# Transfers of q, k and V moved to GpSimd's queue, low parts one step later, and work respread in an attention and expert kernel

## The chip, the cores and the metric

One core of a Trainium2 chip runs the whole program. The core has five engines that run side by side and wait for one another by semaphores: TensorE (PE in the profile; its weight loads are listed as PEld), VectorE (DVE), ScalarE (ACT), GpSimd (POOL) and SyncE (SP), which here only issues transfers between device memory and the core's SBUF. The metric is device time in microseconds from start to end of the program; smaller is better. TensorE's results land in PSUM, which has eight banks per partition; VectorE and ScalarE read them there, GpSimd does not.

## What is computed

Attention for 2 batches, 8 heads, 576 positions and 64 columns per head, with a position bias from a small network; then two mixtures of experts over the 1152 rows of the result, the second with its own gate.

```python
scores = scale * np.matmul(q, k.transpose(0, 1, 3, 2))
h = np.maximum(x @ w1 + b1, 0.0)          # x: log distances over log positions
scores = scores + (h @ w2).transpose(2, 0, 1)[None]
attn = softmax(scores); out = attn @ v
# experts, layer 1 (4) and layer 2 (8); D = 512, F = 1024
for e in range(E):
    h = np.maximum(x @ w1[e], 0.0)
    out += p[:, e:e + 1] * (h @ w2[e])
# layer 2: p from logits x @ w_gate: exp(logits - max), then 8 rounds that
# divide by row sums and by column sums
```

All of it is float32. The expert products are made from split operands: a high part (the value rounded to the form that TensorE takes at full rate) and a low part (the value less its high part), three products for each pair.

## The kernel before

**Attention** runs in 36 units. A unit `u` is a block of 128 query rows (`t`, 0 to 4; block 4 holds the last 64 rows of both batches), a pair of heads (`p`) and, for blocks 0 to 3, a batch (`b`). The order is block 0 (units 0 to 7), block 4 (8 to 11), then 1, 2, 3. The loop over `k` is a software pipeline written out by hand: iteration `k` issues for unit `k` the scores (`emit_S`, line 346), their maximum with the bias added (`emit_max`, line 364 on VectorE) and the exponentials (`emit_exp`, ScalarE); for unit `k-1` the reciprocal of the row sums (`emit_recip2`, line 387, whose input `emit_recip` has GpSimd add, line 383) and its copy `spread` on GpSimd; for `k-2` the transposes (`emit_T`, and `emit_tail` for the last 64 columns and `spread`) and their evacuations (`emit_evac`, lines 416 and 418); for `k-3` the product with V (`emit_P`, line 435) into `po`; for `k-4` the scaled result (`emit_x`, line 445, VectorE). Each engine executes what is issued for it in that order.

**Bias.** 36 groups of 16 rows are made beside the units: hidden values `hids` (mostly VectorE, line 283), a product (line 297), a scaled evacuation to one of three places of `bsts` (ScalarE, line 326), a store to device memory `bd` (SP, line 329); `load_bias` (lines 255 and 256) reads it back shifted as `bt`, in two transfers, four for block 4. Eight groups come before everything else, three more before the first unit, then one per unit up to unit 24.

**Loads.** SP issues all transfers in program order: `load_q` (two per head pair and block, 20 calls), `load_k` (two, 8 calls), `load_v` (three, 4 calls, with a memset on GpSimd), bias stores and loads, and from unit 24 the expert weights (`load_raw`). A transfer whose buffer isn't free, or whose source isn't written, holds up those behind it.

**Experts.** A step `n` is a layer, an expert, a chunk of rows (five row tiles, or four) and a quarter of F. `L1` makes the first product of step `n+1` by Strassen's scheme in seven products and a closing part (`m1`, `m6`, `m2`, `m7`, `m5`, `m4`, `m3`, `last`) over three PSUM banks A, B, C, with VectorE's sums (`u2`, `u3`, line 655) between; a bank is taken again only when it has been read. `L2` makes the second product of step `n` into `y` (line 726). `step` interleaves them in slots, and `at(n, slot, ...)` hangs other work into a slot. `split_raw` splits weights (line 162 on GpSimd, sums on VectorE).

**Operands.** `pieces` makes the seven combinations of the rows that the scheme needs (`X`). Each piece is three parts; a part makes sums on VectorE and calls `split`, which copies the high part on ScalarE (line 99) and at once has another engine subtract for the low part (line 100). Layer 1's first chunk is made in iterations 16 to 34 of attention, its second chunk in steps 0 and 1, layer 2's after layer 1.

**Between the layers** each finished row tile is transposed (`transposed`), gated (`gate`) and split; `sinkhorn` finds the largest logit (`largest`, `turned`, `largest_of_all` at line 831), broadcasts it by a product (`to_all`, line 835), exponentiates, and runs eight rounds.

Of the kernel before, what the change touches and what calls it, by code (L numbers as in the profile page):

```python
# [9 lines left out]
F32 = mybir.dt.float32  # L10
F32R = mybir.dt.float32r
AF = mybir.ActivationFunctionType
ALU = mybir.AluOpType
# [12 lines left out]
WARM = 10  # L26
# [22 lines left out]
def attn_moe_moe(ctx: ExitStack, tc: tile.TileContext, pack, keep, rel, qT, kT, vT, w, out):  # L49
# [40 lines left out]
    def pieces(layer, c):  # L90

        n = CHUNKS[c][1]
        for i in XA:
            X[layer, c, i] = xpools[c].tile([128, 2, 2, n], F32R, tag=f"x{c}{i}", name=f"x{layer}{c}{i}")

        def split(i, src, o, w, lo):
            x = X[layer, c, i]
            hi = x[:, 0, :, o:o + w]
            sc.activation(out=hi, in_=src, func=AF.Copy)
            lo.tensor_tensor(out=x[:, 1, :, o:o + w], in0=src, in1=hi.bitcast(F32), op=ALU.subtract)  # L100

        def piece(k1, c1, k2, c2, w, o):
            h1, h2 = col_tile(k1)[:, :, c1:c1 + w], col_tile(k2)[:, :, c2:c2 + w]
            a11, a12, a21, a22 = h1[:, 0:2], h1[:, 2:4], h2[:, 0:2], h2[:, 2:4]
            t1, t2 = (g1.tile([128, 2, 128], F32, tag=f"t{i}", name=f"t{i}_{layer}{k1}")[:, :, 0:w] for i in range(2))

            def part1(eng, other):
                eng.tensor_tensor(out=t1, in0=a21, in1=a22, op=ALU.add)
                eng.tensor_tensor(out=a21, in0=a11, in1=a21, op=ALU.subtract)
                eng.tensor_tensor(out=t2, in0=t1, in1=a11, op=ALU.subtract)  # L110
                split("A11", a11, o, w, other)

            def part2(eng, other):
                split("A12", a12, o, w, eng)
                eng.tensor_tensor(out=a12, in0=a12, in1=t2, op=ALU.subtract)
                split("A22", a22, o, w, other)
                split("S1", t1, o, w, eng)

            def part3(eng, other):
                split("S2", t2, o, w, eng)  # L120
                split("S3", a21, o, w, eng)
                split("S4", a12, o, w, eng)

            return [part1, part2, part3]

        return [piece(*x) for x in CHUNKS[c][2]]


    NP = F // 256
# [46 lines left out]
    def attention(moe):  # L176
# [17 lines left out]
        V = [atb.tile([128, 5, 2 * B * D], F32, name=f"V{p}") for p in range(4)]  # L194

        def load_v(p):
            sy.dma_start(out=V[p][:, 0:4, :], in_=vT[p, 0:512].rearrange("(j p) x -> p j x", p=128))
            gp.memset(V[p][:, 4, :], 0.0)
            for h in range(2):
                to, of = (x.rearrange("p (b h d) -> p h b d", b=2, h=2)[:, h] for x in (V[p][:, 4, :], vT[p, 512:576]))  # L200
                sy.dma_start(out=to[64 * h:64 * h + 64], in_=of)

        bdram = [dram.tile([H, (128 if t < 4 else 64) + 1, W], F32, name=f"bd{t}") for t in range(5)]

# [7 lines left out]
        def load_k(p, b):  # L212
            i = 2 * p + b
            r = xa.tile([128, 1280], F32, tag=f"x0{XA[i % 4]}", name=f"kr{p}{b}")[:, 0:S]
            for h in range(2):
                sy.dma_start(out=r[64 * h:64 * h + 64], in_=kT[p, b, 0:64, S * h:S * h + S])
            rawk[p, b] = r

        def prep_k(p, b, hi):
# [9 lines left out]
        def load_q(t, p):  # L229
            r = ata.tile([128, 256], F32, tag="qraw", name=f"qr{t}{p}", bufs=3)  # L230
            for h in range(2):
                sy.dma_start(
                    out=r[64 * h:64 * h + 64].rearrange("p (b c) -> p b c", b=2),
                    in_=qT[t, p, 0:64].rearrange("p (b h c) -> p h b c", b=2, h=2)[:, h],
                )
            rawq[t, p] = r
# [214 lines left out]
        kq = [(p, b) for p in range(4) for b in range(2)]  # L451

        gp.memset(ones, 1.0)
        for _ in range(WARM):
            pe.matmul(out=po_all[:, 0, 0:128], lhsT=ones, rhs=ones, start=True, stop=True)
        sy.dma_start(out=cst, in_=pack)
        sy.dma_start(out=T, in_=rel)
        load_q(*tps_[0])
# [43 lines left out]
                load_k(*kq[4])  # L502
                load_q(*tps_[2])

        load_bias(*tps_[0])
        load_bias(*tps_[1])
        load_k(*kq[5])
        load_q(*tps_[3])
        prep_q(*tps_[1])
        prep_k(*kq[2], sc)  # L510
        for _ in range(3):
            groups(1)
            hids(4)
        prep_k(*kq[3], sc)

        ti, work, first_split = 0, [], None
        for k in range(U + 3):
            first = False
            if k < U:
                t, p, b = units[k]  # L520
                first = b == 0
                if first:
                    ti = tps_.index((t, p))
                emit_S(k)
                emit_max(k)
                if k > 0:
                    emit_recip2(k - 1)
                if k >= 4:
                    emit_x(k - 4)
            elif k == U:  # L530
                emit_recip2(k - 1)
                emit_x(k - 4)
                st_sc.close()
                st_a.close()
                moe.open1()
                first_layer = moe.L1(0)
                for fn in first_layer[0:3]:
                    fn()
            if k < U:
                emit_exp(k, 0)  # L540
            if k >= 2 and k - 2 < U:
                emit_T(k - 2)
                emit_evac(k - 2, 0, sc)
            if k < U:
                emit_exp(k, 1)
            if k >= 2 and k - 2 < U:
                emit_evac(k - 2, 2, sc)
            groups(1)
            if k >= 2 and k - 2 < U:
# [27 lines left out]
                ve.reciprocal(psm, psm)  # L577
                ve.tensor_tensor(out=p1, in0=dp, in1=psm.unsqueeze(2).to_broadcast([128, NTT, E1]), op=ALU.mult)
            if k == 15:
                work = [part for p_ in pieces(1, 0) for part in p_]  # L580
            if work and (15 < k < 19 or 22 < k):
                work.pop(0)(ve, gp)
            if k == 24:
# [18 lines left out]
    class Moe:  # L602
# [169 lines left out]
        def turn(self, n, c):  # L772
# [7 lines left out]
            if c == 0:  # L780
                for i, k in enumerate(tiles):
                    self.at(n + 1, 1 + i, lambda k=k: self.transposed(k, "y4"))
                    self.at(n + 1, 2 + i, lambda k=k: self.gate(k, "y4"), False)
                self.at(n + 1, 7, make)
                for i in range(15):
                    self.at(n + 1 + (i + 7) // 8, (i + 7) % 8, lambda i=i: self.parts[i // 3][i % 3](ve, gp))
            else:
                for i, (slot, tag) in enumerate(((6, "A"), (7, "B"), (8, "C"), (8, "A"))):
                    self.at(n + 1, slot, lambda k=tiles[i], tag=tag: self.transposed(k, tag))
                for i, k in enumerate(tiles):  # L790
                    self.at(n + 2, 6 + i, lambda k=k, i=i: self.gate(k, "ABCA"[i]))
                self.at(n + 2, 9, make)
                for i in range(6):
                    self.at(n + 3, i, lambda i=i: self.parts[i // 3][i % 3](ve, gp))
                self.sinkhorn(n + 5)

        def transposed(self, k, tag):
# [17 lines left out]
        def sinkhorn(self, n0):  # L815
# [53 lines left out]
            self.at(n0 - 2, 4, largest)  # L869
            self.at(n0 - 2, 7, turned, False)  # L870
            self.at(n0 - 2, 7, largest_of_all)
            self.at(n0 - 2, 9, to_all, False)
            self.at(n0 - 2, 9, exps)
            for i in range(SINKHORN):
                self.at(n0 + i // 2, 2 + 4 * (i % 2), sums, False)
                self.at(n0 + i // 2, 2 + 4 * (i % 2), lambda i=i: over_cols(i))
# [25 lines left out]
                gran.pop(self.gidx(n))  # L902

        def run(self):
            work = [part for p_ in pieces(1, 1) for part in p_]
            for i, part in enumerate(work):
                self.at(i // 3, 2 + 2 * (i % 3), lambda part=part: part(ve, gp))
            for n in range(self.N):
                self.step(n)

# [73 lines left out]
```

## Time and profile before

| | us |
|---|---|
| median of three runs | 1388.31 (1388.0 to 1389.45) |
| the profiled execution | 1387.5 |
| its span, first to last instruction | 1385.7 |
| TensorE busy in the span | 1339.5 (97%) |
| VectorE, ScalarE, GpSimd busy | 783.9, 517.5, 390.2 |
| mean granted TensorE clock | 0.993 of full speed |

A busy TensorE is not TensorE at its peak: matmuls are pipelined, and their ends are modelled. The granted clock has two levels here, 1.0 (2.4 GHz) and 0.5 (1.2 GHz). Times in a timeline count from the start of the span.

### The profile page before, as it was taken

The page shows a single profiled execution, that of the slowest core. Times are in us where ns is not written, and L with a number is a line of the kernel's source. Part 1 is how long each engine was busy: PE and PEld are TensorE (multiplying, and loading weights), DVE is VectorE, ACT ScalarE, POOL GpSimd, SP SyncE. Part 2 cuts the span into 40 slices and gives each one's busy share as a digit, 9 for nine tenths or more (in the row PEclk, how much of TensorE's full clock was granted, in tenths as well). Part 3 has the DMA queues.
Part 4 walks back from the last instruction along what each step waited for, and adds up shares of the span by engine and source line. Part 5 has one row for each costly group of instructions (what it writes and reads, how often), then busy time and mean ns, then how long its engine had stood idle before and what let it go on. Part 6 is the DMA issues. An engine that isn't in the chain of part 4 may idle for free.

```text
span 1385.7 us, 22442 instructions
## 1 busy us (share of the span) xinstructions
PE 1339.5 (97%) x8763; PEld 1167.2 (84%) x8763; DVE 783.9 (57%) x1775; ACT 517.5 (37%) x1226; POOL 390.2 (28%) x391
## 2 busy tenths in 40 slices
PE   7889888999999999999999999999999999999998
PEld 3576677899899898889888888898988988988987
DVE  7667778454464463585474473664544734635643
ACT  6768774334142241343243241331321422413311
POOL 0111134044062160144062260340530612604400
PEclk9899999999999999999999999999999999999999
DMA  7775521011021020011021030020110210301110
GB/s 208 197 180 143 159 66 61 31 61 62 0 87 37 0 94 29 1 61 62 1 92 31 14 97 12 31 92 0 62 61 1 92 31 26 97 1 35 58 39 31
DMA packets 42170, 84.68 MB, mean 61 GB/s; under 512 B 10320, under 2 KB 17744, under 8 KB 42064
## 3 DMA queue, kind: packets, MB, share of 16 engines
q1 hardware_dynamic: 42064, 83.24, 19.7%
q8 instruction: 69, 1.13, 0.3%
q14 instruction: 37, 0.30, 0.1%
HBM read 69.97 MB, written 13.25 MB: 60 GB/s over the span
## 4 chain that ended last, share of the span: by engine, by line
PE 84%; DVE 7%; ACT 3%; DMA 3%; issue 1%; POOL 1%; SPq 1%; ACTq 0%; DVEq 0%; POOLq 0%
PE y L726 41%; PE B L647 16%; PE A L647 10%; PE C L647 10%; PE po L435 2%; PE sc L346 2%; DVE s L364 2%; ACT s L377 1%; PE bps L297 1%; PE tp L409 1%; DMA bd<-bsts 1%; DMA rawb<-in_w 1%; ACT bsts L326 1%; DMA bt<-bd 1%; ACT at L418 1%
## 5 line engine op out<-in xcount | busy, mean ns | idle before, releaser
L726 PE MATMUL y<-gb,h 128*128 128x512 f32 x2592 | 714.7, 396 | 0.0
L726 PEld LDWEIGHTS y<-gb,h 128*128 128x128 f32 x2592 | 451.5, 188 | 56.0 <-issue 0.2
L162 POOL TENSOR_TENSOR gb<-rawb,gb 128x512 fp32r<-128x512 f32 x94 | 126.7, 1361 | 637.9 <-ACT gb L161 630.8
L655 DVE TENSOR_TENSOR u<-B,s 128x320 f32<-128x320 f32 (+1 forms) x192 | 87.7, 457 | 311.9 <-PE B L647 311.7
L658 ACT ACTIVATE h<-c 128x320 fp32r<-128x320 f32 (+1 forms) x288 | 119.6, 439 | 385.3 <-DVE c L655 383.8
L661 DVE SCALAR_TENSOR_TENSOR h<-c,h 128x320 fp32r<-128x320 f32 (+1 forms) x288 | 170.1, 607 | 53.0 <-ACT h L658 48.1
L162 POOL TENSOR_TENSOR ga<-rawa,ga 128x512 fp32r<-128x512 f32 x94 | 120.5, 1300 | 5.9 <-ACT ga L161 5.8
L655 DVE TENSOR_TENSOR c<-C,u 128x320 f32<-128x320 f32 (+1 forms) x192 | 87.5, 456 | 60.7 <-PE C L647 57.1
L162 POOL TENSOR_TENSOR ga<-wt,ga 128x512 fp32r<-128x512 f32 x94 | 105.4, 1141 | 36.1 <-ACT ga L161 19.2
L669 ACT ACTIVATE s<-A 128x320 f32<-128x320 f32 (+1 forms) x96 | 39.5, 411 | 173.0 <-PE A L647 173.0
L658 ACT ACTIVATE h<-A 128x320 fp32r<-128x320 f32 (+1 forms) x96 | 39.1, 407 | 146.1 <-PE A L647 145.9
L655 DVE TENSOR_TENSOR c<-B,s 128x320 f32<-128x320 f32 (+1 forms) x96 | 43.9, 458 | 82.0 <-PE B L647 80.8
L161 ACT ACTIVATE gb<-rawb 128x512 fp32r<-128x512 f32 x96 | 60.1, 627 | 73.0 <-DMA rawb<-in_w 73.0
L377 ACT ACTIVATE s<-s,stat 128x576 f32<-128x576 f32 x72 | 55.4, 769 | 42.1 <-DVE stat L364 41.2
L435 PEld LDWEIGHTS po<-at,V 128*64 128x64 f32 x800 | 39.3, 137 | 33.7 <-DVE rows L445 32.5
L647 PE MATMUL A<-x20A,ga 128*128 128x320 f32 x384 | 66.9, 309 | 0.0
L647 PE MATMUL B<-x20S,ga 128*128 128x320 f32 x384 | 66.8, 309 | 0.0
L647 PE MATMUL C<-x20S,ga 128*128 128x320 f32 x384 | 66.7, 309 | 0.0
L647 PEld LDWEIGHTS B<-x20S,ga 128*128 128x128 f32 x384 | 61.6, 188 | 5.8
L647 PEld LDWEIGHTS C<-x20S,ga 128*128 128x128 f32 x384 | 61.3, 188 | 5.8
L647 PEld LDWEIGHTS A<-x20A,ga 128*128 128x128 f32 x384 | 61.4, 188 | 5.6
L435 PE MATMUL po<-at,V 128*64 128x128 f32 (+1 forms) x800 | 47.5, 267 | 16.1 <-DVE rows L445 16.1
(173 smaller groups left out, 1904.8 us busy)
## 6 DMA issues: line engine op xcount, KB each, us to landing
rawa<-in_w SPq DMA_DIRECT2D x48, 512.0 KB, 4.0
rawb<-in_w SPq DMA_DIRECT2D x48, 512.0 KB, 4.9
bd<-bsts SPq DMA_DIRECT2D x36, 295.5 KB, 3.4
bt<-bd SPq DMA_DIRECT2D x16, 512.0 KB, 4.3
qr<-in_qT SPq DMA_DIRECT2D x40, 64.0 KB, 3.0
kr<-in_kT SPq DMA_DIRECT2D x16, 144.0 KB, 3.2
V<-in_vT SPq DMA_DIRECT2D x4, 512.0 KB, 4.8
bt<-bd SPq DMA_DIRECT2D x8, 256.0 KB, 4.0
```

The source lines that it names most:

```text
L161: sc.activation(out=z(0), in_=src, func=AF.Copy)
L162: lo.tensor_tensor(out=z(1), in0=src, in1=z(0).bitcast(F32), op=ALU.subtract)
L346: pe.matmul(out=o[h][:, j, 0:288], lhsT=qq[t, p][d, x, 128 * bb:128 * bb + 128], rhs=kk[p, bb][d, y, 288 * j:288 * j + 288], start=i == 0, ...
L364: ve.tensor_tensor_reduce(out=s.rearrange("p (a j) -> p a j", a=2), in0=scps.pop((u, h))[:, :, 0:288], in1=bt[t, p][:, S * h:S * h + S].re ...
L377: sc.activation(out=s, in_=s, func=AF.Exp, scale=-1.0, bias=stat[u][:, h:h + 1], accum_out=stat[u][:, 2 + h:3 + h],)
L435: pe.matmul(out=o[64 * h:64 * h + 64, c0:c0 + n], lhsT=V[p][:, j, col:col + D], rhs=rhs, start=j == 0, stop=j == 4,)
L647: pe.matmul(out=ban[o], lhsT=a, rhs=x[:, z, k, :], start=not more and i == 0, stop=i == 5, skip_group_check=more,)
L655: ve.tensor_tensor(out=t[o], in0=ban[a], in1=t[b], op=ALU.add)
L658: sc.activation(out=h[f][:, 0, half, :], in_=src, func=AF.Relu)
L661: ve.scalar_tensor_tensor(out=h[f][:, 1, half, :], in0=src, scalar=0.0, in1=h[f][:, 0, half, :].bitcast(F32), op0=ALU.max, op1=ALU.subtract,)
L669: sc.activation(out=t["s1"], in_=ban["A"], func=AF.Copy)
L726: pe.matmul(out=self.y[t], lhsT=a, rhs=x, start=g == 0 and f == 0 and i == 0, stop=g == NP - 1 and f == 1 and i == 2,)
```

## The change

Transfers of q, k and V are issued by GpSimd instead of SP. In `pieces` the subtraction for a low part is put aside (`pending`) and issued at the start of the next part (`flush`), so that there is one closing part more; the copies are spread otherwise over the three parts. In the first units TensorE gets products of ones whose result nobody reads (`busy`): eight before unit 0, six after the scores of units 0, 1 and 2. `emit_x` stands ahead of `emit_S`. Once all bias groups are made, one evacuation moves ahead of the second exponential. The first two bias loads come after bias group 8. The parts of layer 1's second chunk go from steps 0 and 1 to steps 1 and 2, with low parts on VectorE alone. The broadcast of the largest logit and the exponentials move from step 34 to step 35, slot 9.

```diff
@@ pieces
+        pending = []
         def split(i, src, o, w, lo):
             sc.activation(out=hi, in_=src, func=AF.Copy)
-            lo.tensor_tensor(out=x[:, 1, :, o:o + w], in0=src, in1=hi.bitcast(F32), op=ALU.subtract)
+            pending.append(lambda: lo.tensor_tensor(out=x[:, 1, :, o:o + w], in0=src, in1=hi.bitcast(F32), op=ALU.subtract))
+        def flush(eng=None, other=None):
+            while pending:
+                pending.pop(0)()
             def part1(eng, other):
+                flush()
                 ...
+                split("A12", a12, o, w, eng)
                 split("A11", a11, o, w, other)
+                split("S1", t1, o, w, eng)
             def part2(eng, other):
-                split("A12", a12, o, w, eng)
+                flush()
                 eng.tensor_tensor(out=a12, in0=a12, in1=t2, op=ALU.subtract)
+                split("S2", t2, o, w, eng)
                 split("A22", a22, o, w, other)
-                split("S1", t1, o, w, eng)
             def part3(eng, other):
-                split("S2", t2, o, w, eng)
+                flush()
                 split("S3", a21, o, w, eng)
                 split("S4", a12, o, w, eng)
-        return [piece(*x) for x in CHUNKS[c][2]]
+        return [part for x in CHUNKS[c][2] for part in piece(*x)] + [flush]
@@ load_v, load_k, load_q (each transfer)
-            sy.dma_start(...)
+            gp.dma_start(...)
@@ before the units
-        load_bias(*tps_[0])
-        load_bias(*tps_[1])
         load_k(*kq[5])
         load_q(*tps_[3])
         prep_q(*tps_[1])
         prep_k(*kq[2], sc)
-        for _ in range(3):
+        for g in range(3):
             groups(1)
             hids(4)
+            if g == 0:
+                load_bias(*tps_[0])
+                load_bias(*tps_[1])
+        busy(8)
         prep_k(*kq[3], sc)
@@ the units
+                if k >= 4:
+                    emit_x(k - 4)
                 emit_S(k)
+                if k < 3:
+                    busy(6)
                 emit_max(k)
                 if k > 0:
                     emit_recip2(k - 1)
-                if k >= 4:
-                    emit_x(k - 4)
             ...
                 emit_evac(k - 2, 0, sc)
+                if made == NGR:
+                    emit_evac(k - 2, 2, sc)
             if k < U:
                 emit_exp(k, 1)
-            if k >= 2 and k - 2 < U:
+            if k >= 2 and k - 2 < U and (k - 2, 2) in tps:
                 emit_evac(k - 2, 2, sc)
@@ Moe.turn: 16 parts instead of 15 for the first chunk, 7 instead of 6 for the second
@@ sinkhorn
-            self.at(n0 - 2, 9, to_all, False)
-            self.at(n0 - 2, 9, exps)
+            self.at(n0 - 1, 9, to_all, False)
+            self.at(n0 - 1, 9, exps)
@@ run
-            for i, part in enumerate(work):
-                self.at(i // 3, 2 + 2 * (i % 3), lambda part=part: part(ve, gp))
+            for i, part in enumerate(pieces(1, 1)):
+                self.at(*((1, 1 + 3 * i) if i < 3 else (2, 2 * i - 5)), lambda part=part: part(ve, ve))
```

## Rows read from the trace of the kernel before

**Rows 1.** Busy time by stretch: stretch, its length, engines (instructions), clock, DMA share, GB/s.
```profile
0.00:58.00 58.00, 42.64 (x353) 23.73 (x354) 41.52 (x108) 37.49 (x77) 4.40 (x17) 0.88 0.71 204
...
156.00:202.00 46.00, 37.26 (x442) 31.31 (x444) 37.17 (x120) 33.32 (x96) 16.07 (x34) 1.00 0.36 111
202.00:250.00 48.00, 41.95 (x280) 36.53 (x277) 38.20 (x69) 22.11 (x54) 19.27 (x18) 0.96 0.21 66
...
575.00:725.00 150.00, 143.89 (x849) 127.17 (x848) 99.97 (x268) 62.43 (x162) 59.23 (x56) 0.99 0.15 47
...
sum 1385.00, PE 1339.53 PEld 1167.19 DVE 783.95 ACT 517.52 POOL 390.19; mean PE 167.44 PEld 145.90 DVE 97.99 ACT 64.69 POOL 48.77
```

**Rows 2.** Who waited for whom: us in total, times, longest us.
```profile
PE po L435 <- DVE rows L445: 16.1, 18, 2.2
...
DVE s L364 <- PE sc L346: 11.5, 15, 1.8
```

**Rows 3.** Timeline 26 to 37 us: start, length, what, idle before and its releaser.
```profile
26.50 1.05 PE L346 MATMUL sc<-kk,qq 64*128 64x288 f32 x11 [0.92 <-ACT bsts L326]
...
28.53 1.24 SPq L232 DMA_DIRECT2D qr<-in_qT  x2
29.34 0.76 DVE L364 CUSTOM_DVE_ANT_0 s<-sc,bt 128x576 f32<-128x576 f32 x1 [1.44 <-DMA bt<-bd]
29.87 6.50 SPq L329 DMA_DIRECT2D bd<-bsts  x4
...
34.78 1.05 ACT L326 ACTIVATE bsts<-bps,cst 128x16 f32<-128x16 f32 x2 [3.01 <-DMA bd<-bsts]
...
35.88 1.81 PE L346 MATMUL sc<-kk,qq 64*128 64x288 f32 x11 [3.03 <-ACT bsts L326]
```

**Rows 4.** Timeline of a later unit: eight transposes, of the fill products' shape.
```profile
62.81 1.04 PE L409 MATMUL tp<-kept,s 128*128 128x128 f32 x8
```

**Rows 5.** Busy time in the stretch of the lower clock, columns as in the first group.
```profile
28.00:41.60 13.60, 8.40 (x51) 4.60 (x52) 7.24 (x21) 6.42 (x14) 1.57 (x4) 0.50 0.70 201
```

**Rows 6.** GpSimd's sums (ns min/median/max), then sums and tails of units 0 and 4.
```profile
L383 POOL TENSOR_SCALAR stat<-stat x36: 213/219/625, 31.9 to 202.7; 128x2 f32<-128x2 f32 x36
...
31.86 0.62 POOL L383 TENSOR_SCALAR stat<-stat 128x2 f32<-128x2 f32 x1 [30.94 <-ACT s L377]
...
41.28 0.42 PE L398 MATMUL sc<-kept,spread 128*128 128x128 f32 x1
...
57.05 0.35 POOL L383 TENSOR_SCALAR stat<-stat 128x2 f32<-128x2 f32 x1 [1.11 <-ACT s L377]
...
62.70 0.27 PE L398 MATMUL sc<-kept,spread 128*128 128x128 f32 x1
```

**Rows 7.** Timeline, VectorE's maxima of units 10 and 12.
```profile
84.20 0.76 DVE L364 CUSTOM_DVE_ANT_0 s<-sc,bt 128x576 f32<-128x576 f32 x1 [2.97 <-DMA bt<-bd]
...
96.11 0.76 DVE L364 CUSTOM_DVE_ANT_0 s<-sc,bt 128x576 f32<-128x576 f32 x1 [2.91 <-DMA bt<-bd]
```

**Rows 8.** Timeline, steps 0 and 1 of the expert layers.
```profile
226.22 1.14 PE L647 MATMUL B<-x10A,ga 128*128 128x320 f32 x6 [1.71 <-DVE u L655]
...
240.04 1.45 POOL L162 TENSOR_TENSOR ga<-rawa,ga 128x512 fp32r<-128x512 f32 x1
240.29 1.48 DVE L108 TENSOR_TENSOR t<-rows 128x256 f32<-128x256 f32 x1
...
243.51 1.94 PE L647 MATMUL B<-x10A,ga 128*128 128x320 f32 x6 [3.31 <-DVE u L655]
...
244.53 0.42 DVE L115 TENSOR_TENSOR rows<-rows,t 128x256 f32<-128x256 f32 x1
```

**Rows 9.** Groups in 157 to 202 us: busy, mean ns, idle before.
```profile
L435 PE MATMUL po<-at,V 128*64 128x128 f32 x212 | 14.0, 278 | 8.7 <-DVE rows L445 8.7
```

**Rows 10.** Timeline of TensorE around the broadcast of the largest logit.
```profile
662.63 0.38 PE L835 MATMUL B<-m,ones 1*128 1x1 f32 x2 [1.84 <-DVE m L831]
662.94 1.65 PE L726 MATMUL y<-gb,h 128*128 128x512 f32 x3
```

## What I predict, before the result is known

> **What bounds the kernel now.** I read the table by stages first: busy time of each engine in stretches of the span [rows 1]. TensorE is busy for 1339.5 of 1385.7 us; of the 46 us that it stands still, 36 lie in four places: 58.0 - 42.6 = 15.4 us in the start of attention, 46.0 - 37.3 = 8.7 us in its last units, 48.0 - 42.0 = 6.0 us at the entry to the first expert layer, 150.0 - 143.9 = 6.1 us in the passage between the layers. The long expert stretches behind them have nothing to give. Next, who ended these waits [rows 2]: the largest single one is the attention product `po` waiting 16.1 us, in 18 pieces, for VectorE's line 445 (`emit_x`). Last the timeline of each place, in the order below. The change touches all four.
>
> **Start, unit 0: SP relieved.** The store of bias group 8 leaves at 29.87 us, because two bias loads, two transfers of k and two of q stand before it in SP's queue; ScalarE then waits 3.01 us for that store's buffer (`bsts` has three places) and S(1) on TensorE 3.03 us for ScalarE [rows 3]. After the change k and q are not in that queue, and the store stands before the bias loads. New in front of S(0) are 8 fill products of two instructions each; an instruction of the same shape takes 1.04/8 = 0.13 us in mid-attention [rows 4], so 8 x 2 x 0.13 = 2.1 us (twice that at the 1.2 GHz level). S(0) ends at 27.55 now, and would end near 28.4; maximum(0) starts at 28.5 instead of 29.34, for SP is about 1.6 us earlier with its bias. Without the two waits of 3 us S(1) starts near 32.5 instead of 35.88: -3.4 us. The fills behind S(0) to S(2), 6 x 2 x 0.13 = 1.6 us each, fall into stretches in which TensorE waits for maximum or ScalarE; I put +0.5 us for what sticks out (0 to 4.8, were that cover gone).
>
> **Clock.** From 28.0 to 41.6 us the granted clock is 0.50, the 1.2 GHz level, and TensorE is busy for 8.4 of these 13.6 us, with the two waits of 3 us in them [rows 5]. S(1), S(2) and a group of bias products lie on the path there, each about 0.8 us dearer than later. If the fills and the shorter waits keep 2.4 GHz, I gain up to 2.3 us; I take a third, -0.8.
>
> **GpSimd as a queue.** 68 transfers move (20 of q x 2, 8 of k x 2, 4 of V x 3). No row shows a transfer issued by GpSimd. From below, SP's price: 1.24/2 = 0.62 us each [rows 3]; from above one whole tensor operation of GpSimd, 1.45 us [rows 8]. I take 1.0, between them. Behind them on GpSimd stand the sums for the reciprocal and `spread`, for which VectorE and the tail transposes of TensorE wait. Behind unit 0's sum stand seven transfers: the sum ends at 32.5 now and near 31.6 then, the tail wants `spread` at 41.28 now and near 37.9 then [rows 6]. 31.6 + 7 + 0.7 = 39.3: cost +1.4 us (0 at 0.62, +4.6 at 1.45). Behind units 2, 4 and 6 stand five, and 5.3 us lie between sum and tail (57.40 to 62.70); in other units two at most. Loads are asked for a unit or more before use, so at these prices lateness of their own costs nothing. The start: -3.4 + 0.5 - 0.8 + 1.4 = -2.3.
>
> **The middle.** In row block 4 each unit has its own q and bias load; two q transfers, 1.24 us, stand before the bias load on SP, and maximum waits 2.97 and 2.91 us for it [rows 7]. Two times 1.2 us come back: -2.4. Moving `emit_x` ahead of `emit_S` takes P(k-3) off maximum(k); but in these units S(k+1) waits for ScalarE (exponentials, evacuations) until nearly the same time, so of the other waits I take -0.6. Sum -3.0, bounds 0 and 16.1 - 8.7 = -7.4 [rows 2, 9].
>
> **Last units (156 to 202 us).** Of the wait for line 445, 8.7 us lie here [rows 9]. It goes: x(k-4) runs ahead of maximum(k), and VectorE no longer stands waiting for ScalarE's copy before each low part. What is late next is VectorE itself, busy 37.2 of 46.0 us, as long as TensorE's 37.3 [rows 1]; two engines equally full in one chain will not both reach 100%. I take -5.0 (bounds -2 and -8.7).
>
> **Entry (202 to 250 us).** TensorE waits 1.71 and 3.31 us for `u`, because VectorE is behind. A subtraction of a part costs it 1.48 us beside a GpSimd operation of 1.45, and 0.42 without [rows 8]. Step 0 loses its three parts, so the 1.71 goes. Step 1 keeps three, with the same seven subtractions before `u3` but without two GpSimd operations of low parts beside them: -1.3 of 3.31. Step 2 gets the other four, with no weight split beside them: 13 x 0.42 = 5.5 us on a VectorE that otherwise has slack, no cost (half of it, 2.7, if not). Sum -3.0 (+1 to -6.7, the latter with the clock of that place).
>
> **Passage.** The parts of layer 2 keep their operations, VectorE is full beside them: -0.7 (+0.5 to -4.3). The broadcast of the largest logit waits 1.84 us for line 831, and the three products behind it take 1.65 us, twice the usual, at the 1.2 GHz level [rows 10]. One step later nobody waits for it; but the next product needs the bank `A` that line 831 reads, so half a microsecond stays. With some 1.7 us of lost clock: -2.7 (-0.8 to -3.5). The exponentials then end about 1 us before the first column sums want them.
>
> **Sum.** -2.3 - 3.0 - 5.0 - 3.0 - 0.7 - 2.7 = -16.7 us. The profiled execution took 1387.5 us around its span of 1385.7, 0.8 below the median: 1388.3 - 16.7 = 1371.6, say 1372.
>
> **A rule against it.** GpSimd's sum takes 0.22 us in the median and up to 0.63 [rows 6]: beside VectorE's work it can lose some 0.4 us. The Trainium skill, SBUF — State Buffer, Who interferes with whom, says that VectorE's copy, cast and tensor-scalar forms in a two-port mode lock GpSimd out, and starve the descriptors of transfers that it issues; another section there has one of 0.62 us taking 3.1. By that figure, an estimate, seven transfers take 22 us and the change would lose; no run here shows it yet.
>
> **Rivals.** (1) ScalarE takes the place of the waits removed; it is busy 33.3 of 46 us in the last units [rows 1], exponentials in series. Then start -1.5, middle -1.3, last units -2, entry -1.5, passage -1.5: -7.8, 1380.5. For: SP's relief does not shorten ScalarE's chain. Against: its own waits there are for VectorE. (2) Starved transfers: each loses those 0.4 us two or three times, 2 us instead of 1.0. Unit 0: 31.6 + 14.7 = 46.3 against 37.9, +8.4; units 2, 4, 6: 10.7 against 5.3, three times, +16 less what later slack gives back, say 8. So +16 in place of +1.4: -18.1 + 16 = -2, 1386. The skill page above speaks for this one. (3) Slower: building a transfer holds VectorE as GpSimd's subtractions do, by 1.48 - 0.42 = 1.06 us at most. Before its maxima VectorE waits 11.5 us for TensorE [rows 2], which would hide as much. It decides from (11.5 + 17)/68 = 0.42 us per transfer; at 0.65, 44 - 11.5 - 17 = +16, 1404. For: VectorE is 70 to 80% busy where all 68 lie. Against: the rows show such holding only where both engines read two tiles. (4) The fills do not hold the clock: 0.8 to 3 us, inside the range.
>
> **Chances.** Forecast 0.60, rival 1 0.22, rival 2 0.09, rival 3 0.09. About 0.2%, 2.8 us, is what can be told from no change. Faster: 0.60 + 0.22 = 0.82, within: rival 2 but for a rest, 0.08; slower: 0.10. Low end: twice the gains of last units and entry and the clock kept, 1361. High end: rival 1 with GpSimd's +4.6, 1385. This leaves out rivals 2 and 3.
>
> **What would show it.** Right: no wait of `po` for line 445, and units 3.9 us apart at the end; S(1) before 33 us; no wait at line 835; no wait for `u` in step 0. Wrong: maxima, `hids` or casts that grow beside GpSimd's transfers; tails waiting for `spread`; the `po` waits back as equal waits of S for ScalarE's evacuations.

## The result, and the profile after

The changed kernel takes 1363.71 us in the median of four executions (1362.6 to 1366.74); the kernel before took 1388.15 us beside it. The ratio is 0.9827, 95% interval 0.9807 to 0.9847: 24 us faster, where 16 were forecast. The time lies inside the stated range, in its lower part.

The profiled execution took 1366.7 us (span 1365.0). A second profile, taken with the last experiments, has 1363.85 us (span 1362.1), which is the median; where stages are added up, that one is used. First the stretches that the forecast started from, in the first profile (columns as in [rows 1]):

```profile
0.00:58.00 58.00, 48.20 (x416) 29.92 (x416) 43.49 (x114) 39.17 (x82) 28.88 (x55) 0.98 0.73 209
156.00:202.00 46.00, 45.31 (x518) 39.36 (x518) 40.72 (x125) 35.67 (x98) 16.53 (x35) 1.00 0.30 93
202.00:250.00 48.00, 47.27 (x273) 41.86 (x267) 34.49 (x69) 19.10 (x48) 15.56 (x12) 1.00 0.21 66
575.00:725.00 150.00, 146.05 (x859) 130.26 (x860) 96.49 (x249) 62.24 (x147) 58.13 (x52) 1.00 0.16 52
28.00:41.60 13.60, 11.01 (x110) 8.22 (x110) 10.39 (x29) 7.41 (x17) 7.98 (x14) 1.00 0.81 257
```

TensorE's idle time falls from 15.4 to 9.8 us in the first stretch, from 8.7 to 0.7 in the second, from 6.0 to 0.7 in the third and from 6.1 to 4.0 in the fourth [rows 1]. The last line answers to [rows 5]: the granted clock is 1.00, the 2.4 GHz level, where it was 0.50. GpSimd is now busy for 28.9 us of the first 58, in place of 4.4: transfers that it issues are in its rows. Of the first stretch's smaller idle time part is no gain: the fills count as busy, and products of ones take 11.1 of its 48.2 us, in place of 4.0 of 42.6.

The stretches are fixed in time while the work moves, so the gain of a stage is better read between landmarks of the timeline. Before against the second profile: maximum of unit 7, maximum of unit 25, first expert product, first product `turn` of the passage, last instruction.

| stage, up to | before | after | gain | forecast |
|---|---|---|---|---|
| start, maximum of unit 7 | 66.89 | 64.75 | 2.1 | 2.3 |
| middle, maximum of unit 25 | 156.93 | 150.11 | 4.7 | 3.0 |
| last units, first expert product | 202.62 | 188.12 | 7.7 | 5.0 |
| entry and layer 1, first `turn` | 562.18 | 540.32 | 7.4 | 3.0 |
| passage and layer 2, end | 1385.71 | 1362.07 | 1.8 | 3.4 |

The gains add up to 23.6 us, which is also 1387.5 - 1363.85 of the two executions. Against the first profile they are 0.8, 4.4, 7.7, 7.3 and 0.6: the last units and the entry hold, the start and the passage differ by more than a microsecond from one execution to the other. What still waits on TensorE, in the second profile (us in total, times, longest):

```profile
PE sc L356 <- ACT at L428: 4.9, 6, 1.5
PE C L667 <- DVE c L675: 1.9, 1, 1.9
...
PE B L667 <- DVE u L675: 0.9, 2, 0.6
...
PE po L445 <- DVE rows L455: 0.7, 1, 0.7
```

(`emit_x` is line 455 now, the product with V 445, scores 356, maximum 374, evacuations 428, low parts 103.) The 16.1 us in 18 pieces of [rows 2] are one piece of 0.7. The waits of 1.71 and 3.31 us for `u` in steps 0 and 1 [rows 8] are gone. The scores wait 4.9 us for ScalarE's evacuations; before, these waits were 1.6 and 1.2 us at units 3 and 4, 2.8 in all, and came ahead of the `po` waits. This is the first rival's mechanism, and it costs little here.

The start, in the first profile (answers to [rows 3]):

```profile
28.14 10.74 SPq L339 DMA_DIRECT2D bd<-bsts  x4
...
30.32 0.76 DVE L374 CUSTOM_DVE_ANT_0 s<-sc,bt 128x576 f32<-128x576 f32 x1 [1.78 <-DMA bt<-bd]
...
33.74 1.05 PE L356 MATMUL sc<-kk,qq 64*128 64x288 f32 x11 [1.09 <-ACT bsts L336]
```

S(1) starts at 33.74 in place of 35.88 (32.42 in the second profile; 32.5 was forecast) and takes 1.05 us in place of 1.81: it has the full clock. Its wait for ScalarE is 1.09 us, not 3.03.

GpSimd's queue in the first two units, second profile, and then the durations of the 40 transfers of q (ns, minimum, median, maximum):

```profile
31.52 0.62 POOL L393 TENSOR_SCALAR stat<-stat 128x2 f32<-128x2 f32 x1 [11.64 <-ACT s L387]
32.20 1.22 POOL L242 DMA_DIRECT2D qr<-in_qT  x2
33.42 1.06 POOL L226 DMA_DIRECT2D kr<-in_kT  x2
34.47 0.81 POOL L207 DMA_DIRECT2D V<-in_vT  x1
35.24 0.49 POOL L208 MEMSET V<- 128x256 f32 x1
...
37.37 0.30 POOL L399 COPY spread<-stat 128x128 f32<-128x128 f32 x1
```

```profile
L242 POOL DMA_DIRECT2D qr<-in_qT x40: 599/620/839, 1.3 to 158.0; - x40
```

Those of k have a median of 0.54, those of V of 0.61 and 0.80, none of the 68 is over 0.84 us: about SP's price (0.62). The seven transfers behind unit 0's sum end at 37.37, and the tail waits 0.58 us for `spread`.

### The profile page after: what moved, and what is told of

It reads as the page before. It is cut to its first block, busy times and chain, and to the rows that moved or that the text cites. A ratio compares the mean times of both kernels' runs of the same rounds, so it can differ in the third digit from the quotient of the medians.

```text
span 1365.0 us, 22554 instructions
## 1 busy us (share of the span) xinstructions
PE 1340.4 (98%) x8815; PEld 1170.1 (86%) x8815; DVE 785.1 (58%) x1779; ACT 517.0 (38%) x1226; POOL 431.3 (32%) x455
## 4 chain that ended last, share of the span: by engine, by line
PE 90%; DVE 5%; ACT 3%; DMA 1%; issue 1%; SPq 0%; DVEq 0%; ACTq 0%
PE y L746 43%; PE B L667 16%; PE A L667 11%; PE C L667 11%; PE po L445 2%; PE sc L356 2%; PE tp L419 2%; PE bps L307 1%; ACT s L387 1%; DMA bt<-bd 1%; DVE s L374 1%; ACT bsts L336 1%; ACT at L428 0%; PE turn L832 0%; DMA bd<-bsts 0%
## 5 line engine op out<-in xcount | busy, mean ns | idle before, releaser
L675 DVE TENSOR_TENSOR c<-B,s 128x320 f32<-128x320 f32 (+1 forms) x96 | 43.9, 458 | 82.0 <-PE B L667 80.9
L374 DVE CUSTOM_DVE_ANT_0 s<-sc,bt 128x576 f32<-128x576 f32 x72 | 51.5, 753 | 16.0 <-PE sc L356 9.9
L667 PEld LDWEIGHTS A<-x21A,ga 128*128 128x128 f32 x384 | 54.4, 188 | 6.4 <-issue 1.2
```

The source lines that it names most:

```text
L374: ve.tensor_tensor_reduce(out=s.rearrange("p (a j) -> p a j", a=2), in0=scps.pop((u, h))[:, :, 0:288], in1=bt[t, p][:, S * h:S * h + S].re ...
L667: pe.matmul(out=ban[o], lhsT=a, rhs=x[:, z, k, :], start=not more and i == 0, stop=i == 5, skip_group_check=more,)
L675: ve.tensor_tensor(out=t[o], in0=ban[a], in1=t[b], op=ALU.add)
```

## Experiments

Medians are of four executions (five of the changed kernel in experiment 1, ten for the two kernels built from the one before); ratios are against the kernel before on the same chip. The changed kernel itself has 0.9827 and 0.9829 in its two measurements, so an experiment's effect is the difference from 0.9829, times 1388 us; an interval reaches some 2 to 3 us to either side. None of them can be told to be faster than the changed kernel.

**1. The changed kernel once more.**

> The changed kernel once more, beside the next three on one chip. Theory (the granted clock fell for some 3 us at 56 to 60 us in its first profile and in few other executions, which costs 1.6 us): most executions 1362 to 1363.5, some near 1365 to 1366.5; the median at 1363. Rival (the spread of 4 us comes from elsewhere, such as transfers that land at other times): executions of full clock lie as far apart as the others.

1363.85 us in the median (1362.43 to 1367.14), 0.9829 (0.9813 to 0.9845). Each of the two holds in part. The fall costs what the theory took: from the maximum of unit 1 to that of unit 7 it takes 31.1 us in the two profiles of this kernel, which have it (a granted clock of 0.92 over 44 to 66 us), and 29.3 to 29.5 us in the four profiles of experiments 6 to 8 that don't (1.00). But it is not rare, and it doesn't set the spread: of the nine executions of this kernel, five with a mean clock of 0.999 or 1.0 lie 2.4 us apart, four with 0.997 or 0.998 4.5 us (1362.61 to 1367.14). The second profile has the fall too, to a mean of 0.60 at 54 to 58 us, and is still 2.9 us shorter than the first. Of these, 1.3 us lie in front of the first maximum, which waits 0.74 us for its bias instead of 1.78; and 1.2 are a wait for `u` that the first profile has at 698.20 us and the second has not. Unit 25 to the passage agree within 0.1 us. So a difference of under 3 us between two single profiles, taken as a whole, says nothing; the stages are what can be compared.

**2. Loads of q, k and V.** Back on SP in the changed kernel, and on GpSimd as the only edit of the kernel before:

```diff
-                gp.dma_start(
+                sy.dma_start(
```

> The changed kernel with the transfers of q, k and V issued by SP again, all else kept. Theory (SP's queue holds up the bias transfers): the bias loads and the store of group 8 again stand behind k and q, so S(1) loses most of the 2.5 us that it gained, and row block 4 its 2 x 1.2 us: +3 to +5 us, 1367 to 1369. Rival 1 (the place of the first two bias loads alone gave the start): S(1) stays near 33.7 us and only row block 4 comes back, +1 to +2.5, 1365 to 1366. Rival 2 (issuing on GpSimd has a price of its own there, for its sums and copies wait behind 68 transfers): -0.5 to -2, 1362.

> The kernel before, with the transfers of q, k and V on GpSimd as the only edit; the first bias loads stay ahead of group 8. Theory: the two waits of 3 us (ScalarE for the store, S(1) for ScalarE) shrink to about 1 us and the two maxima of row block 4 lose 1.2 us of wait each: -3 to -5, 1383 to 1385. Rival (the store is held up by the bias loads in front of it, which wait for their source, not by k and q): S(1) stays near 37 us, only row block 4 gains, -1 to -2.5, 1386 to 1387.

Back on SP: 1368.02 us, 0.9848 (0.9833 to 0.9862), +2.6. GpSimd alone: 1385.98 us, 0.9984 (0.9975 to 0.9994), -2.2 (-3.5 to -0.8). Against the second profile the first of them is 2.9 us later at unit 1 and 3.0 at unit 7; GpSimd alone is 1.3 us earlier at unit 1 and gains 1.5 us more in row block 4 (29.22 to 27.77 us from unit 7 to unit 12). Unit 1 lies at 33.6 to 35.1 us in the eight profiles with these loads on GpSimd and the same 26 fills, so that of the 2.9 us there only 1.4 to 2.9 are the queue's; the 3.0 at unit 7 are 0.8 against the one of the eight that is latest there. That SP's queue costs time is shown in both directions, but the sizes are those that the theory had as its lowest, or less, and by time alone the rival of the second run would do as well. S(1) decides: it starts at 34.91 and 34.57 us, neither near 37 nor at 33.7. Rival 2 of the first run, that issuing on GpSimd costs, falls: the time rises when they go back. Why GpSimd alone gains less at the start than was expected is seen in its profile:

```profile
31.07 2.15 PE L297 MATMUL bps<-hidS,w2n 128*32 128x288 f32 x16 [2.77 <-DVE stat L364]
...
34.57 1.80 PE L346 MATMUL sc<-kk,qq 64*128 64x288 f32 x11 [0.82 <-ACT bsts L326]
```

The wait of 3.03 us is 0.82, but the product ahead of S(1) takes 2.15 us and S(1) itself 1.80: the lower clock has stayed.

Row block 4 is where the forecast put 2.4 us. With the loads back on SP it takes 27.7 us from unit 7 to unit 12, against 26.9 to 27.5 in the same eight profiles, so the move of the transfers is worth 0.2 to 0.8 us of it there, and 1.5 us as the only edit.

**3. Fills.**

```diff
-        busy(8)
...
-                if k < 3:
-                    busy(6)
```

> The changed kernel without the 26 fill products before and behind the first scores. Theory (they hold the clock): the granted clock is 0.50 again for some 8 to 13 us after 28 us, which costs 1.5 to 2.5 us against some 0.5 us of fills that stuck out: +1 to +2, 1365 to 1366. Rival (the waits of 3 us that SP's relief took away were what let the clock fall): the clock stays at 1.00, and without the fills the time is the same or up to 1 us less, 1363.

1365.72 us, 0.9831 (0.9815 to 0.9848): no difference that can be told. But the clock falls:

```profile
28.00:41.60 13.60, 9.66 (x67) 4.83 (x67) 9.55 (x25) 6.72 (x15) 6.98 (x13) 0.75 0.79 231
43.00:49.00 6.00, 5.37 (x43) 3.77 (x45) 3.78 (x11) 4.47 (x12) 4.08 (x8) 0.72 0.86 237
```

All four executions have a mean granted clock of 0.994 to 0.996, the nine of the changed kernel 0.997 to 1.000. Unit 1 is 2.1 us later than in the second profile (1.0 of it lies in front of the first maximum), unit 7 0.5, unit 35 1.6; against the first profile unit 1 is 0.8 later and unit 7 0.8 earlier. So the fills help to hold the clock, and it is worth at most a microsecond or two. They don't do it alone: with the fills but the loads back on SP (experiment 2) the stretch from 28 us is the same 0.75,

```profile
28.00:41.60 13.60, 10.51 (x76) 7.45 (x75) 7.39 (x21) 5.88 (x14) 1.57 (x4) 0.75 0.73 228
```

and one profile with both, that of the old evacuation (experiment 6), has 0.87 there.

**4. More fills.**

```diff
-                if k < 3:
+                if k < 8:
                     busy(6)
```

> The changed kernel with six fill products behind the scores of units 0 to 7 instead of 0 to 2. Theory (the clock of the first 60 us hangs on TensorE's waits in units 3 to 6): no fall of the clock in any execution, fills mostly in waits of 1.2 to 1.5 us of these units: -1 to -0.3, 1362 to 1363. Rival (the fills stand in front of the bias product and the transposes, for which ScalarE waits, and lengthen each unit): 5 x 0.3 to 0.8 us, +1.5 to +4, 1365 to 1367.5.

1370.63 us, 0.9874 (0.986 to 0.9888), +6. The rival is right. Up to unit 4 the profile is that of the second one; from unit 5 on each unit is longer, and unit 12 is 5.0 us late. What waits, over 44 to 100 us:

```profile
DVE hids L293 <- PE bps L307: 10.2, 8, 1.9
```

In the second profile VectorE waits 3.9 us there (44 to 97 us): the fills stand in front of the bias product. And from unit 4 on the bank that they write is read by the scaled result, so that they wait themselves, 1.6 us in one piece. The changed kernel stops them where nothing reads the bank yet.

**5. The scaled result first, as the only edit of the kernel before.**

```diff
+                if k >= 4:
+                    emit_x(k - 4)
                 emit_S(k)
                 emit_max(k)
...
-                if k >= 4:
-                    emit_x(k - 4)
```

> The kernel before, with the scaled result of unit k-4 issued ahead of the scores of unit k as the only edit. Theory (the order on VectorE carries the last units): the 16.1 us in which the product with V waits for this step fall under 4 us, units 26 to 35 come 3.5 to 3.7 us apart in place of 4.27: -6 to -9, 1379 to 1382. Rival (VectorE is held by ScalarE's copies in the parts of the operands, so that the step only waits elsewhere): the wait goes, but units at the end stay over 4.0 us apart with the lost time in front of the scores: -1 to -3, 1385 to 1387.

1388.08 us, 1.0000 (0.9991 to 1.0009). Nothing, less even than the rival's 1 to 3 us, though the wait that the forecast called the largest is nearly gone (0.7 us in these units) and units 26 to 35 come 4.2 us apart. Its last units (156.9 to 201 us), and then the scores over the whole span:

```profile
ACT s L377 <- DVE stat L364: 12.7, 10, 2.2
...
PE tl L397 <- ACT at L418: 5.7, 8, 0.7
DVE x10S L100 <- ACT x10S L99: 4.8, 4, 1.4
DVE x10A L100 <- ACT x10A L99: 3.2, 3, 1.4
```

```profile
PE sc L346 <- ACT at L418: 10.3, 10, 1.9
```

The time has moved to ScalarE: the transposes `tl` wait 5.7 us for it, and the scores 10.3 us, where they waited 2.8 before; ScalarE's exponentials wait 12.7 us for VectorE's maxima; and VectorE stands 8.0 us for ScalarE's copies of the high parts. I read that as a ring of three engines, in which the order of `emit_x` has no part.

**6. The three edits that could open the ring, each taken out of the changed kernel.**

```diff
-            pending.append(lambda: lo.tensor_tensor(...))
+            lo.tensor_tensor(...)
```

> The changed kernel with each low part subtracted at once behind its copy, all else kept. Theory (both edits of order carry the last units, this one only spares VectorE its short waits for ScalarE's copies): VectorE stands some 0.3 us for a copy in each of the parts, which is slack in the units but not at the entry and in the passage: +1 to +3, 1365 to 1367. Rival (this edit carries the last units): units 26 to 35 4.1 to 4.3 us apart, +6 to +8, 1370 to 1372.

```diff
-                if k >= 4:
-                    emit_x(k - 4)
                 emit_S(k)
...
                 if k > 0:
                     emit_recip2(k - 1)
+                if k >= 4:
+                    emit_x(k - 4)
```

> The changed kernel with the scaled result of unit k-4 issued behind the maximum of unit k again, all else kept. Theory (the last units need both edits: this order on VectorE, and on ScalarE the evacuation ahead of the second exponential; alone the order only moved the wait to the transposes of the tail): the product with V waits for this step again, 10 pieces of 0.5 to 1.2 us in units 26 to 35 and some earlier: +6 to +9, 1370 to 1373. Rival (the low parts one part behind carry the last units, the order is worth nothing, as in the kernel before): within 1.5 us, 1362 to 1365.

```diff
-                if made == NGR:
-                    emit_evac(k - 2, 2, sc)
```

> The changed kernel with the evacuation of the tail behind the second exponential in all units, all else kept. Theory (both edits are needed): transposes of the tail wait 0.7 us for ScalarE in 8 to 10 of the last units, as they did when the order alone was changed: +4 to +7, 1368 to 1371, and units 26 to 35 come about 4.2 us apart. Rival (the low parts one part behind have made room on ScalarE and VectorE): within 1.5 us, 1362 to 1365.

Low parts at once: 1378.88 us, 0.9941 (0.9923 to 0.9960), +15.5, far above what either theory gave. The result behind: 1370.41 us, 0.9881 (0.9860 to 0.9902), +7. The evacuation behind: 1365.10 us, 0.9842 (0.9820 to 0.9865), +1.8, not told from nothing; its profile has two of the forecast eight to ten waits, 0.38 and 0.73 us. So the order is needed, as its theory has it, but its partner is the low parts and not the evacuation. (With the low parts at once the copies are still spread over the parts in the new way; that spread was not tried by itself.)

From the maximum of unit 25 to the first expert product it takes 45.7 us before, 38.0 in the second profile, 44.3 with the low parts at once, 45.0 with the result behind, 43.9 in the kernel of experiment 5 and 39.1 with the old evacuation. So the order and the low parts, each without the other, gain 0.7 to 1.8 us there, and both together 7.7. Why they need each other is in the waits. Low parts at once, 153.9 to 198.2 us:

```profile
ACT s L387 <- DVE stat L374: 12.7, 11, 3.2
...
DVE x10S L103 <- ACT x10S L102: 7.7, 7, 1.4
...
PE po L445 <- DVE rows L455: 5.3, 9, 2.4
...
DVE x10A L103 <- ACT x10A L102: 1.3, 2, 0.7
```

The scaled result behind the maximum, 149.1 to 194.1 us:

```profile
ACT s L387 <- DVE stat L374: 11.4, 11, 2.1
DVE s L374 <- PE sc L356: 10.2, 9, 1.6
...
PE po L445 <- DVE rows L455: 7.1, 11, 1.5
```

And the changed kernel, second profile, 150.1 to 188.1 us:

```profile
ACT s L387 <- DVE stat L374: 5.3, 7, 2.2
DVE s L374 <- PE sc L356: 2.0, 4, 0.7
...
PE po L445 <- DVE rows L455: 0.7, 1, 0.7
```

With the low parts at once, VectorE loses 9.0 us to copies that ScalarE makes late. With the result behind, the copies cost nothing, but VectorE waits 10.2 us for scores, which stand behind the product with V, which waits 7.1 us for the result that VectorE makes after the maximum: a ring of two. With either ring left, units 26 to 35 come 4.2 to 4.3 us apart on average; with both open, 3.6 us.

The low parts also matter elsewhere: at once, units 12 to 25 take 62.5 us in place of 58.4 (60.8 before), and from the first expert product to `turn` 4.7 us more. In units 12 to 25 the order by itself costs time: with the result behind the maximum they take 57.5 us in place of 58.4, and in the kernel of experiment 5 61.7 in place of 60.8.

**7. The entry.** The parts of the second chunk at their old slots, and GpSimd's low parts at the new ones:

```diff
-                self.at(*((1, 1 + 3 * i) if i < 3 else (2, 2 * i - 5)), ...: part(ve, ve))
+                self.at(i // 3, 2 + 2 * (i % 3), ...: part(ve, ve))
```

> The changed kernel with the seven parts of the second chunk of layer 1 in steps 0 and 1 again (slots 2, 4 and 6 of each, the last at the start of step 2), low parts on VectorE alone. Theory (the place carries the entry): three parts more lie in step 0 beside GpSimd's weight splits, and the waits of 1.71 and 3.31 us for u come back for the greater part: +3 to +5, and with the clock that falls behind the longer one up to +7, 1367 to 1371. Rival (GpSimd's low parts, which hold VectorE, were the cost, the place is none): +0 to +1.5, 1363 to 1365.

```diff
-                self.at(..., lambda part=part: part(ve, ve))
+                self.at(..., lambda part=part: part(ve, gp))
```

> The changed kernel with GpSimd making one low part in each part of layer 1's second chunk again (in steps 1 and 2), all else kept. Theory (a subtraction of GpSimd beside one of VectorE makes both 1.4 us instead of 0.4; in steps 1 and 2 VectorE has 13 of them, four lows move): +0.5 to +2.5, 1364 to 1366, with u waited for again in step 1. Rival (the place alone made the entry's gain; VectorE has slack there): within 0.5 us.

Old slots: 1368.87 us, 0.9866 (0.9848 to 0.9884), +5. GpSimd's low parts: 1363.66 us, 0.9828 (0.9814 to 0.9842), nothing. So the place is worth some 5 us by the medians and 3 by its stage, and the engine of the low parts nothing that can be told once the place has changed. The stage from the first expert product to `turn` is 3.1 us longer with the old slots than in the second profile, with these waits:

```profile
210.70 1.15 PE L667 MATMUL B<-x10A,ga 128*128 128x320 f32 x6 [1.01 <-DVE u L675]
225.20 1.12 PE L667 MATMUL B<-x10A,ga 128*128 128x320 f32 x6 [0.76 <-DVE u L675]
```

They were 1.71 and 3.31 us before, with the lower clock behind the second [rows 8]; here there is no fall, so less than "the greater part" comes back. Of the 7.4 us of this stage, then, 3.1 go with the place and 4.3 with the low parts one part behind or on VectorE. Low parts at once, at the new slots, cost 4.7 us of this stage (experiment 6), which points at the first of the two; at the old slots they were not taken apart.

**8. The broadcast of the largest logit one step earlier again.**

```diff
-            self.at(n0 - 1, 9, to_all, False)
-            self.at(n0 - 1, 9, exps)
+            self.at(n0 - 2, 9, to_all, False)
+            self.at(n0 - 2, 9, exps)
```

> The changed kernel with the broadcast of the largest logit and the exponentials one step earlier again, all else kept. Theory: the broadcast waits some 1.8 us for the maximum over the largest logits again and the granted clock falls behind it for 3 us, against 0.8 us that the next product waits for the bank now: +1.5 to +3, 1364.5 to 1366. Rival (the later exponentials and rounds push a wait of 1.2 us for u into the step with the column sums, which takes the gain): within 1 us, and that wait is gone.

1365.13 us, 0.9832 (0.9819 to 0.9846), +0.4: no difference. Its profile, and the place in the first profile of the changed kernel:

```profile
641.12 0.38 PE L855 MATMUL B<-m,ones 1*128 1x1 f32 x2 [1.40 <-DVE m L851]
641.43 0.96 PE L746 MATMUL y<-gb,h 128*128 128x512 f32 x3
```

```profile
642.41 0.95 PE L667 MATMUL A<-x21A,ga 128*128 128x256 f32 x6 [0.80 <-DVE m L851]
```

The move saves 1.40 - 0.80 = 0.6 us of waiting. The three products behind take 0.96 us, not 1.65 [rows 10]: with the wait at 1.40 us instead of 1.84 the granted clock stays at 1.00. The rival is half right: the gain is under 1 us, but the wait of 1.2 us for `u` is there as well.

## Why the prediction was right or wrong, step by step

**Start: mechanism right, the size in part by luck.** 2.1 us against 2.3, but 0.8 in the first profile. The store leaves earlier and S(1) waits 1.09 us in place of 3.03; "S(1) before 33 us" holds in the second profile (32.42) and not in the first (33.74). At unit 1 the gain is 3.8 us in the second and 2.5 in the first; 1.7 us of it is gone again by unit 7 in both. The clock, of whose 2.3 us a third was taken, holds through the whole stretch of [rows 5], and falls for 3 us later, at 54 to 58 us or at 56 to 60. That fall, worth 1.6 us, was not in the forecast.

**GpSimd as a queue: right in mechanism, the price too high.** 1.0 us per transfer was taken between 0.62 and 1.45; it is 0.54 to 0.80 in the median, near the lower end, and the cost at the tail is 0.58 us, not 1.4. Rivals 2 and 3 fall by rows: no transfer takes more than 0.84 us, and the maxima beside transfers last 0.76 us as before. The starving that the Trainium skill (SBUF — State Buffer, Who interferes with whom) warns of is not seen in any of the 68 rows. Nor is it seen in the landings: those of q come 2.8 us after the issue in the median and 4.3 at most, where SP's came 3.0 and 6.0 after.

**Middle: one term right by its sum alone, one mis-sized.** Row block 4 gives 2.25 us (29.22 to 26.97 from unit 7 to unit 12) against 2.4, but the two q transfers ahead of the bias load, to which all of it was put down, are worth 0.2 to 1.5 (experiment 2); what gives the rest was not isolated. "Of the other waits I take -0.6" was wrong: units 12 to 25 give 2.4. The low parts at once cost 4.1 us there. VectorE's waits for copies, which the forecast had not counted in the middle, were 4.1 us before (96.1 to 156.9 us), and the second profile has none there; the new order of `emit_x` takes 0.9 us back (experiment 6).

```profile
DVE x10A L100 <- ACT x10A L99: 3.1, 2, 1.7
...
DVE x10S L100 <- ACT x10S L99: 1.0, 1, 1.0
```

**Last units: mechanism right, the size wrong, and with it the reason for the size.** Both causes were named: the result ahead of the maximum, and copies that VectorE stood waiting for. But the gain was then cut to 5.0 because VectorE was "busy 37.2 of 46.0 us, as long as TensorE's", so that it would be late next. That was a wrong reading of the row. VectorE's idle time was mostly time in which it was held up, and it could be had back. From the maximum of unit 25 to the first expert product it is idle for 45.7 - 36.3 = 9.4 us, and 6.8 of these are waits for copies, 1.5 for scores:

```profile
156.90:202.60 45.70, 36.96 (x443) 30.86 (x441) 36.30 (x118) 33.61 (x96) 15.61 (x33) 1.00 0.36 111
```

```profile
PE po L435 <- DVE rows L445: 8.7, 11, 1.5
...
DVE x10S L100 <- ACT x10S L99: 4.0, 4, 1.2
DVE x10A L100 <- ACT x10A L99: 2.8, 3, 1.2
...
DVE s L364 <- PE sc L346: 1.5, 2, 1.1
```

With the waits gone, both engines run nearly full: TensorE 37.32 and VectorE 36.09 of 38.00 us:

```profile
150.10:188.10 38.00, 37.32 (x450) 31.83 (x450) 36.09 (x116) 32.54 (x94) 17.72 (x38) 1.00 0.45 135
```

"Two engines equally full in one chain will not both reach 100%" was said without a row, and it kept back little: they reach 98% and 95%. Experiments 5 and 6 also show what the forecast had not seen: the edits don't add up, the order or the low parts without the other is worth 0.7 to 1.8 us in this stage.

**Entry: the term that failed by most, 7.4 us against 3.0.** The wait of 1.71 went, as forecast. Of the 3.31 only 1.3 were taken, "with the same seven subtractions before `u3`"; in truth nothing is left, and the 3 us at the lower clock behind it went too. The sums ahead of `u` are the same, but at slots 1, 4 and 7 those of the last part fall between GpSimd's weight splits and take 0.42 us each, where the first of them took 1.48 [rows 8]; first profile, step 1:

```profile
234.41 0.41 DVE L116 TENSOR_TENSOR t<-rows 128x256 f32<-128x256 f32 x1
...
235.19 0.42 DVE L118 TENSOR_TENSOR t<-t,rows 128x256 f32<-128x256 f32 x1
...
235.83 0.49 DVE L675 TENSOR_TENSOR u<-B,s 128x320 f32<-128x320 f32 x1 [0.22 <-PE B L667]
```

`u` now waits for TensorE. The short sums are not the work of the place alone: at the old slots, with the low parts one part behind and on VectorE, the same three take 0.42, 0.43 and 0.42 us, and TensorE still waits 0.76 us. GpSimd's own low parts, to which the 1.3 was put down, cost nothing that can be told at the new place (experiment 7). The lower bound, -6.7, had the clock in it and was closer, though the stage went beyond it.

**Passage: forecast too large, 1.8 against 3.4** (0.6 in the first profile). The broadcast's move is worth 0.6 us in the profile and nothing that can be measured; a wait of 1.9 us for `c` has come in its first steps, where 1.25 and 0.71 were before. Why the wait for the maximum is 1.40 us and not 1.84 when only the broadcast is put back wasn't tried.

**Rival 1, ScalarE in the place of the waits removed,** had 0.22 and is what the one edit alone does (experiment 5): there TensorE's waits did go over to ScalarE. In the whole change ScalarE's own waits for VectorE's maxima fell with VectorE's for the copies, from 11.9 to 5.3 us in the last units.

The sum was 16.7 us and the stages gave 23.6: middle, last units and entry are 8.8 us short together, passage and start 1.8 us too large, so that the total is nearer than its terms. Behind most of the shortfall of the first two are VectorE's waits for copies, 4.1 and 6.8 us, which stood in the trace with their sizes: not counted in the one, read as an engine that is full in the other. The low end of the range counts 0.8 us of the clock twice: 1371.6 - 5.0 - 3.0 - 1.5 is 1362, not 1361; the measured median lies above both.

## What to carry to other kernels

Before an engine is called full, look at what its idle time in that stretch waits for: if it is the other engine of a pair that also waits for it, the idle time is a ring and not slack, and opening it can give back most of it. Such a ring was opened here by issuing the dependent half one stage later, and where two rings run through the same engine, one edit alone may measure as nothing. Transfers moved to a queue with room cost there what they had cost in the old queue, and no row showed contention.

## What the runs showed that was not expected

- Filling TensorE to hold its clock was worth little here: the fall from 28 us, without the fills, takes the mean clock of an execution from some 0.998 to 0.995, and no time that can be told.
- The clock fell at 54 to 58 us in the second profile to a mean of 0.60, right behind a stretch in which TensorE was busy for 2.53 of 4.00 us:

```profile
50.00:54.00 4.00, 2.53 (x33) 1.69 (x27) 3.96 (x14) 2.86 (x7) 0.94 (x3) 0.98 0.66 200
54.00:58.00 4.00, 4.00 (x27) 3.00 (x25) 1.61 (x5) 3.05 (x9) 3.44 (x7) 0.60 0.59 135
```

- Executions of one program on one core differ by 4.7 us (1362.43 to 1367.14) and two profiles show it in pieces of 1.2 to 1.3 us that come and go: the first bias transfer lands earlier, a wait for `u` is there or not. What sets them was not tried.
